# A transformer block's opening in another order, and its features dealt to partitions in fours

## The chip, the core and the metric

The kernel runs on one core of a Trainium2 chip. The metric is the time of one execution on the device, in microseconds, as the median of several runs. The engines are TensorE (PE, with its weight loads shown apart as PEld), VectorE (DVE), ScalarE (ACT), GpSimd (POOL) and SyncE (SP), which issues all transfers. Each engine executes its own list of instructions in order.

## The reference

A layer norm feeds attention with one shared key and value head, and an MLP with the mish activation; both are added to the input.

```
S, D, H, Dh, F = 2048, 512, 32, 16, 1792        # all float32
xn = (x - mean(x)) / sqrt(var(x) + 1e-5)
q, k, v = xn @ wq, xn @ wk, xn @ wv              # q: 32 heads of 16; k, v: one head
o = softmax(q @ k.T / 4) @ v                     # per head
h = xn @ w1 + b1
out = x + o @ wo + (h * tanh(softplus(h))) @ w2
```

## The kernel before

All engines' orders are written by hand; nothing is scheduled by a tool. The 2048 tokens form four chunks of 512 (c = 0 to 3), each of four tiles of 128 tokens by 512 features. Products of full precision are made of rounded parts: an operand is split in a high part (a copy that rounds) and a low part (the difference), and a product is three matmuls per 128 features, high by high, high by low and low by high.

The main part is run off a long table of letters (the loop over `word`): per step first scores whose maxima VectorE takes, second scores whose exponentials ScalarE takes, sums with the values, and halves of the MLP's products. The change does not touch the table. It touches the opening, the block under the pool `first`, up to `flush(*(("q", ...` near L876.

The opening loads tokens and weights, normalises the chunks, transposes them, makes keys and values, projects queries, and takes the 32 score maxima of the first unit of heads (u = 0).

- `load_tokens` (L311) loads a chunk's four tiles. `statistics` (L316) runs two instructions per tile on VectorE (L322, L323) and, after all four, `rooted` (L327): variance and mean in four columns (L329, L330) on VectorE, a logarithm and an exponential (L331, L332) on ScalarE. `root` (L335) refines the result with four small instructions, and `normalise` (L342) or `normalise_on_two` (L348) applies it, the latter with two tiles on VectorE and two on ScalarE (L354).
- `first_transposes` (L356) and `transposes` (L368) turn the normalised tiles on TensorE: the token tile is the weights, an identity the moving operand. There are 16 transposes for chunk 0 (L361) and 48 for the others (L375). ScalarE copies the high part out (L363, L377), and VectorE (chunks 0 and 1) or POOL (2 and 3) makes the low part (L387).
- `keys_values` (L408) multiplies with `wkv`; its rest, tagged `("v", c)`, transposes the values on VectorE (L427, four instructions, and a memset L428) when the tag is flushed.
- `queries` (L437) projects 128 of the 512 query columns. ScalarE evicts each (L448, L449), POOL makes the low part (L452), and SyncE stores it (L458, L459). There are four buffers `q`. The first one goes straight into `QS` with six transfers (L469). All weights of a query or MLP product come through three buffers `raw` (L254): a new load waits until the block that used the buffer before is split.
- `first_maxima` (L504) makes two score tiles (L490) and VectorE reduces them (L507). A loop over 32 of them (L832) puts transposes, keys, values and query products of later chunks between them. `fill_slot` makes so many matmuls of the next query or MLP product.
- After the 32, `place_maxima` (L516) writes the maxima through DRAM into two rows of `QS`: a store (L530) and two loads (L532), which wait for it on SyncE.

What sets the order around the change is the program text of the opening, since `later` and `flush` only move a step to the place where its tag is flushed.

Of the kernel before, what the change touches and what calls it, by code (L numbers as in the profile page):

```python
# [178 lines left out]
def attention_and_mlp(ctx: ExitStack, tc: tile.TileContext, x, wq, wk, wv, wo, w1, b1, w2, out):  # L179
# [73 lines left out]
    def raw_block(kind, i):  # L253
        raw = work.tile([P, D], F32, tag="raw", name=f"raw_{kind}{i}", bufs=RAWS)  # L254
        if kind in ("w1", "wq"):
            src = {"w1": w1, "wq": wq}[kind][:, i * P : (i + 1) * P].rearrange("(t p) f -> p t f", p=P)
            SP.dma_start(out=raw.rearrange("p (t f) -> p t f", t=DT), in_=src)
# [58 lines left out]
    def statistics(c, some=range(NT)):  # L316
        if some[0] == 0:
            ST[c] = first.tile([P, NT, 6], F32, tag="st", name=f"st{c}", bufs=2)
            MV[c] = first.tile([P, NT, 2], F32, tag="mv", name=f"mv{c}", bufs=2)
        st = ST[c]  # L320
        for t in some:
            DVE.bn_stats(out=st[:, t], in_=XS[c, t])  # L322
            DVE.bn_aggr(out=MV[c][:, t], in_=st[:, t])  # L323
        if len(some) == NT:
            rooted(c)
# [6 lines left out]
        ACT.activation(y, z, AF.Exp, scale=-0.5)  # L332
        ROOT[c] = v, y, z, m

    def root(c):  # L335
        v, y, z, m = ROOT[c]
        DVE.tensor_tensor(out=z, in0=y, in1=y, op=ALU.mult)
        DVE.tensor_tensor(out=z, in0=z, in1=v, op=ALU.mult)
        DVE.tensor_scalar(z, z, -0.5, 1.5, op0=ALU.mult, op1=ALU.add)
        DVE.tensor_tensor(out=y, in0=y, in1=z, op=ALU.mult)  # L340

    def normalise(c, engine, some=range(NT)):  # L342
        v, y, z, mean = ROOT[c]
        for t in some:
            x, m, r = XS[c, t], mean[:, t : t + 1], y[:, t : t + 1]
            engine.tensor_scalar(x, x, m, r, op0=ALU.add, op1=ALU.mult)

    def normalise_on_two(c):  # L348
        v, y, z, mean = ROOT[c]
        DVE.tensor_tensor(out=z, in0=y, in1=mean, op=ALU.mult)  # L350
        normalise(c, DVE, range(2))
        for t in range(2, NT):
            x, b, r = XS[c, t], z[:, t : t + 1], y[:, t : t + 1]
            ACT.activation(x, x, AF.Identity, bias=b, scale=r)  # L354

    def first_transposes():  # L356
        xt, FLAT[0] = x_tile(0, work)
        pts = [pair_bank(f"xt0_{k}") for k in range(2)]
        for t in (0, 2, 1, 3):
            for d in range(DT):  # L360
                PE.transpose(pts[d // 2][:, d % 2, t * P : (t + 1) * P], XS[0, t][:, d * P : (d + 1) * P], ident)  # L361
        for d in range(DT):
            ACT.activation(xt[:, 0, d], pts[d // 2][:, d % 2], AF.Copy)  # L363
            if d % 2:
                hi, lo = (xt[:, k, d - 1 : d + 1] for k in range(2))
                later(0, lambda hi=hi, lo=lo, pt=pts[d // 2]: below(DVE, lo, pt, hi), ("lo", 0))

    def transposes(c):  # L368
        xt, FLAT[c] = x_tile(c, first if c else work)
        n = 2 if c < 2 else 1  # L370
        for d in range(0, DT, n):
            pt = pair_bank(f"xt{c}_{d}")[:, :n]
            for a in range(n):
                for t in range(NT):
                    PE.transpose(pt[:, a, t * P : (t + 1) * P], XS[c, t][:, (d + a) * P : (d + a + 1) * P], ident)  # L375
            hi, lo = xt[:, 0, d : d + n], xt[:, 1, d : d + n]
            ACT.activation(hi, pt, AF.Copy)  # L377
            if c < 2:
                later(0, lambda hi=hi, lo=lo, pt=pt: below(DVE, lo, pt, hi), ("lo", c))
            else:  # L380
                x = slot_tile()
                ACT.activation(x, pt, AF.Copy)
                later(0, lambda hi=hi, lo=lo, x=x: below(POOL, lo, x, hi), ("lo", c))
            yield
# [131 lines left out]
    def place_maxima(u):  # L516
        m = work.tile([P, 2, 2, HG // 2 * NT], F32R, tag="mhl", name=f"mhl{u}", bufs=2)
        mt = work.tile([P, 32], F32, tag="mt", name=f"mt{u}", bufs=2)
        hi, lo = m[:, :, 0], m[:, :, 1]
        DVE.tensor_reduce(out=hi, in_=NMR[u][:, :, :, :1], axis=AX.X, op=ALU.max)  # L520
        DVE.tensor_reduce(
            out=NMR[u][:, :, :, 1], in_=hi.bitcast(F32).unsqueeze(3), axis=AX.X, op=ALU.max, negate=True
        )
        with nc.allow_low_precision(reason="one exact difference, rounded as it is written"):
            DVE.tensor_reduce(out=lo, in_=NMR[u], axis=AX.X, op=ALU.add)
        DVE.transpose(out=mt, in_=m.rearrange("p a k n -> p (a k n)").bitcast(F32))

        def send():
            d = scratch.tile([4, HG // 2 * NT, P], F32, tag="m", name=f"m{u}_dram", bufs=2)
            SP.dma_start(out=d.rearrange("r n (g k) -> g (r n) k", g=4), in_=mt)  # L530
            for a in range(2):
                SP.dma_start(  # L532
                    out=QS[u][a * 64 + 48 : a * 64 + 50].bitcast(F32),
                    in_=d[2 * a : 2 * a + 2].rearrange("r (pair t) k -> r pair (t k)", pair=2),
                )

        if u:
            return send
        send()

    PT = {}

# [188 lines left out]
    with tc.tile_pool(name="first", bufs=1) as first:  # L731
        load_tokens(0)
        wkv_raw = first.tile([P, DT, 2 * DH], F32, name="wkv_raw")
        for i, w in enumerate((wk, wv)):
            SP.dma_start(out=wkv_raw[:, :, i * DH : (i + 1) * DH], in_=w.rearrange("(t p) f -> p t f", p=P))
        first_queries = Piece(queries(0, 0))
        load_tokens(1)
        request("w1", 0, WB[0])
# [11 lines left out]
        def clear(*tiles):  # L750
            for t in tiles:
                t = t.rearrange("p a n -> p (a n)") if len(t.shape) == 3 else t
                ACT.activation(t, zero.to_broadcast(list(t.shape)), AF.Copy)
# [7 lines left out]
        def run(generator):  # L761
            for _ in generator:
                pass
# [334 lines left out]
```

## Time and profile before

| | us |
|---|---|
| median of three runs | 1558.04 (1556.52 to 1558.55) |
| the profiled execution | 1556.3 |
| its span, first to last instruction | 1554.5 |
| TensorE busy in the span | 1540.8 (99%) |
| VectorE, ScalarE, POOL busy | 1347.5, 1344.8, 861.0 |

A row of the timeline gives the start in us from the beginning of the span, the length, the engine, the line of the kernel, the operation, what it writes and reads, and how many instructions were merged. In brackets stands the idle time before it with what ended that. A row of the groups gives count, busy time, mean ns of one, and the idle time in front. The granted TensorE clock is 1.00 over the whole opening.

### The profile page before, as it was taken

To read this page: it belongs to the slowest core of one execution; us is meant where nothing else is said; L and a number is where in the kernel's file an instruction comes from. 1 tells how busy PE (TensorE), PEld (TensorE's weight loads), DVE (VectorE), ACT (ScalarE), POOL (GpSimd) and SP (SyncE) were. 2 spreads that over 40 slices of the span, in tenths; PEclk is the share of its full clock that TensorE was granted. 3 is DMA by queue.
4 is the path that set the end of the run, shared out by engine and by line. 5 is a ranking of instruction groups with operands and counts; after the bars stand their busy time and mean duration, and the time that the engine had idled before them with its cause. 6 is when DMAs were issued, how large, how long until landed. Compare 5 with 4: busy or idle time off the path is not lost.

```text
span 1554.5 us, 30222 instructions
## 1 busy us (share of the span) xinstructions
PE 1540.8 (99%) x11554; PEld 849.9 (55%) x11554; DVE 1347.5 (87%) x2291; ACT 1344.8 (87%) x2391; POOL 861.0 (55%) x749
## 2 busy tenths in 40 slices
PE   9899999999999999999999999999999999999998
PEld 7565554555555455545554555555555555555555
DVE  7759998899899898999988899999989999998841
ACT  6559999999899989897889989898889998888996
POOL 6657765677565455633556465734255663443652
PEclk9999999999999999999999999999999999999999
DMA  6773322332222222123333221213321221223120
GB/s 211 275 272 103 120 93 77 107 102 97 87 100 72 86 86 73 45 92 106 106 113 108 68 73 59 88 54 145 93 80 51 92 78 55 97 79 120 36 96 28
DMA packets 69399, 152.53 MB, mean 98 GB/s; under 512 B 12774, under 2 KB 22054, under 8 KB 68870
## 3 DMA queue, kind: packets, MB, share of 16 engines
q1 hardware_dynamic: 69254, 150.60, 29.3%
q8 instruction: 91, 1.49, 0.4%
q14 instruction: 54, 0.44, 0.1%
HBM read 98.51 MB, written 51.64 MB: 97 GB/s over the span
## 4 chain that ended last, share of the span: by engine, by line
PE 95%; POOL 1%; DVE 1%; ACT 1%; issue 1%; DMA 0%; SPq 0%; POOLq 0%; ACTq 0%; DVEq 0%
PE banks L556 32%; PE banks L926 23%; PE banks L552 19%; PE banks L490 18%; PE banks L699 1%; PE banks L412 1%; DVE nm L507 1%; PE banks L638 1%; PE banks L743 1%; DMA q_dram<-q 0%; POOL q L452 0%; PE banks L375 0%; ACT q L448 0%; DVE ysb L628 0%; POOL tn L679 0%
## 5 line engine op out<-in xcount | busy, mean ns | idle before, releaser
L502 DVE TENSOR_REDUCE nm<-banks 128x1 f32<-128x512 f32 x1984 | 1241.2, 683 | 131.2 <-PE banks L490 88.0
L991 ACT ACTIVATE pt<-banks 128x512 f32<-128x512 f32 x1594 | 858.3, 604 | 104.3 <-PE banks L552 49.8
L490 PE MATMUL banks<-KS,QS 48*128 48x512 f32 x2048 | 688.0, 423 | 2.5 <-DVE nm L507 2.2
L552 PE MATMUL banks<-QS,KS 64*128 64x512 f32 x2048 | 677.1, 417 | 0.2 <-ACT ty L936 0.2
L556 PE MATMUL banks<-pt,V 128*32 128x512 f32 x4096 | 536.0, 603 | 0.0
L552 PEld LDWEIGHTS banks<-QS,KS 64*128 64x128 f32 x2048 | 329.8, 185 | 224.5 <-DVE nm L502 110.4
L490 PEld LDWEIGHTS banks<-KS,QS 48*128 48x128 f32 x2048 | 329.2, 184 | 203.2 <-DVE nm L502 95.3
L926 PE MATMUL banks<-ring,act 64*128 64x512 f32 x1344 | 330.3, 397 | 0.1
L926 PE MATMUL banks<-X,wblk 64*128 64x512 f32 x1296 | 328.3, 396 | 0.3
L983 ACT ACTIVATE pt<-banks 128x1024 f32<-128x1024 f32 x227 | 230.7, 1027 | 37.1 <-PE banks L552 22.0
L926 PEld LDWEIGHTS banks<-X,wblk 64*128 64x128 f32 x1296 | 213.2, 185 | 28.8 <-issue 10.3
L926 PEld LDWEIGHTS banks<-ring,act 64*128 64x128 f32 x1344 | 211.5, 185 | 31.8 <-issue 11.4
L937 POOL TENSOR_TENSOR ysb<-ysb,ty 128x512 f32<-128x512 f32 x80 | 102.8, 1286 | 162.2 <-ACT ty L936 162.2
L556 PEld LDWEIGHTS banks<-pt,V 128*32 128x32 f32 x4096 | 85.9, 108 | 176.5 <-issue 167.5
L996 POOL TENSOR_SCALAR tu<-tu 128x512 f32<-128x512 f32 x54 | 80.3, 1487 | 125.5 <-ACT tu L995 125.4
L679 POOL TENSOR_TENSOR tn<-tn,tr 128x512 f32<-128x512 f32 x54 | 69.4, 1285 | 126.9 <-ACT tr L1001 126.9
L241 POOL TENSOR_TENSOR act<-th,act 128x512 fp32r<-128x512 f32 x56 | 72.1, 1287 | 99.8 <-ACT act L240 84.6
L682 POOL TENSOR_TENSOR th<-th,tn 128x512 f32<-128x512 f32 x56 | 72.2, 1290 | 0.0
L681 POOL TENSOR_TENSOR tz<-tz,tn 128x512 f32<-128x512 f32 x54 | 69.6, 1288 | 4.5
L998 POOL TENSOR_TENSOR tn<-tn,tu 128x512 f32<-128x512 f32 x54 | 69.5, 1287 | 4.5
L683 POOL TENSOR_TENSOR th<-th,tz 128x512 f32<-128x512 f32 x54 | 69.5, 1287 | 4.2
L926 PE MATMUL banks<-ring,ohl 64*128 64x512 f32 x288 | 64.3, 396 | 0.0
(112 smaller groups left out, 958.1 us busy)
## 6 DMA issues: line engine op xcount, KB each, us to landing
wblk<-w_dram SPq DMA_DIRECT2D x42, 512.0 KB
ring<-w_dram SPq DMA_DIRECT2D x42, 512.0 KB
QS<-q_dram SPq DMA_DIRECT2D x62, 192.0 KB
q_dram<-q SPq DMA_DIRECT2D x16, 512.0 KB
o_dram<-ov SPq DMA_DIRECT2D x31, 256.0 KB
raw_w<-in_B_w_dram SPq DMA_DIRECT2D x28, 256.0 KB
w_dram<-wblk SPq DMA_DIRECT2D x14, 512.0 KB
w_dram<-ring SPq DMA_DIRECT2D x14, 512.0 KB
```

The source lines that it names most:

```text
L241: POOL.tensor_tensor(out=lo, in0=src, in1=hi.bitcast(F32), op=ALU.subtract)
L490: PE.matmul(tile, QS[u][rows, pair, qt * P : (qt + 1) * P], KS[rows, kc * CT : (kc + 1) * CT], start=True, stop=True,)
L502: DVE.tensor_reduce(out=m[:, a : a + 1], in_=tile, axis=AX.X, op=ALU.max)
L552: PE.matmul(bank, KS[rows, kt * P : (kt + 1) * P], QS[u][rows, pair], start=True, stop=True)
L556: PE.matmul(BANK[7][h * 32 : (h + 1) * 32], V[:, kt], PT.pop((u * KT + kt) * HG + h), start=kt == 0, stop=kt == KT - 1,)
L681: POOL.tensor_tensor(out=z, in0=z, in1=n, op=ALU.subtract)
L682: POOL.tensor_tensor(out=h, in0=h, in1=n, op=ALU.mult)
L926: PE.matmul(self.p, w[rows], x[rows], start=self.first, stop=not any(self.todo))
L937: POOL.tensor_tensor(out=YS[t], in0=YS[t], in1=ty, op=ALU.add)
L983: ACT.activation(slots[slot // 2], banks[:, bank : bank + 2], AF.Exp, scale=SCALE)
L991: ACT.activation(PT[n], BANK[bank], AF.Exp, scale=SCALE)
L996: POOL.tensor_scalar_min(tu, tu, U_MAX)
```

## The change

*Features.* Tokens are loaded as before, a token to a partition. The weights with D rows (wk, wv, wq, w1) are loaded so that a partition holds four neighbouring rows instead of four rows 128 apart, and a transpose takes every fourth feature of the tile instead of 128 neighbours. So both operands agree as to which feature lies where.

*Order.* All three `QS` tiles are cleared at the start. Chunk 1's statistics are cut in two around chunk 0's low part; three of its tiles are normalised on VectorE, one on ScalarE. The second block of w1 is split behind that. Chunk 3's statistics move ahead of the maxima, two and two around chunk 1's low part, and its root follows the second maximum. The roots of chunks 2 and 3 run on POOL. The values are transposed behind maxima 7, 9 and 15 and behind all 32. The ones for `KS` are sent at maximum 22 instead of 26. The loads of the maxima follow their store after two fills of 12 matmuls.

```diff
-            src = {...}[kind][:, i * P : (i + 1) * P].rearrange("(t p) f -> p t f", p=P)
+            src = {...}[kind][:, i * P : (i + 1) * P].rearrange("(p t) f -> p t f", p=P)
...
-    def root(c):
+    def root(c, engine):
...
-    def normalise_on_two(c):
+    def normalise_on_two(c, n):
...
-                PE.transpose(pts[d // 2][...], XS[0, t][:, d * P : (d + 1) * P], ident)
+                PE.transpose(pts[d // 2][...], XS[0, t].rearrange("p (n d) -> p d n", d=DT)[:, d], ident)
...
-                    PE.transpose(pt[...], XS[c, t][:, (d + a) * P : (d + a + 1) * P], ident)
+                    PE.transpose(pt[...], XS[c, t].rearrange("p (n d) -> p d n", d=DT)[:, d + a], ident)
...
         if u:
-            return send
-        send()
+            return lambda: load(store())
+        d = store()
+        return lambda: load(d)
...
-            SP.dma_start(out=wkv_raw[...], in_=w.rearrange("(t p) f -> p t f", p=P))
+            SP.dma_start(out=wkv_raw[...], in_=w.rearrange("(p t) f -> p t f", p=P))
...
+        clear(*QT)
...
-        root(0)
-        normalise_on_two(0)
+        root(0, DVE)
+        normalise_on_two(0, 2)
...
-        statistics(1)
+        statistics(1, range(2))
         flush(("lo", 0))
-        split_block()
-        clear(*QT[:2])
+        statistics(1, range(2, NT))
+        rooted(1)
         run(first_keys)
...
-        root(1)
-        normalise_on_two(1)
+        root(1, DVE)
+        normalise_on_two(1, 3)
+        split_block()
...
-        clear(*QT[2:])
         statistics(2)
+        statistics(3, range(2))
         flush(("lo", 1))
         fill_slot(12)
-        root(2)
+        root(2, POOL)
         normalise(2, POOL)
+        statistics(3, range(2, NT))
...
-            if i < NT:
-                statistics(3, range(i, i + 1))
-            if i == NT + 1:
+            if i == 1:
                 rooted(3)
-            if i == NT + 3:
-                root(3)
+            if i == 7:
+                root(3, POOL)
                 normalise(3, POOL)
...
-            if i == 26:
+            if i == 22:
...
-            if i in (8, 12, 18, 22):
-                flush(("v", (8, 12, 18, 22).index(i)))
+            if i in (7, 9, 15):
+                flush(("v", (7, 9, 15).index(i)))
...
-        place_maxima(0)
-        for _ in range(NC * DT):
+        load_maxima = place_maxima(0)
+        flush(("v", 3))
+        for k in range(NC * DT):
             fill_slots(12)
+            if k == 1:
+                load_maxima()
```

Three places in the engines' lists follow. A row gives the line, the operation, what it writes and reads, its size, and how often it repeats. The numbers behind the names tell tiles apart.

VectorE around the start of the maxima, before (X_356 is chunk 1 transposed, z, v and y with 390 to 392 are chunk 2's root, pt_84 and pt_85 hold chunk 3's tokens):

```order
L387 TENSOR_TENSOR X_356<-banks,X_356 128x1024 x2
L337 TENSOR_TENSOR z_392<-y_391 128x4
L338 TENSOR_TENSOR z_392<-z_392,v_390 128x4
L339 TENSOR_SCALAR z_392<-z_392 128x4
L340 TENSOR_TENSOR y_391<-y_391,z_392 128x4
L507 TENSOR_REDUCE nm_441<-banks 128x2
L322 BN_STATS st_445<-pt_84 128x6
L323 BN_AGGR mv_446<-st_445 128x2
L507 TENSOR_REDUCE nm_441<-banks 128x2
```

VectorE at the same place in the change:

```order
L322 BN_STATS st_398<-pt_84 128x6
L323 BN_AGGR mv_399<-st_398 128x2
L387 TENSOR_TENSOR X_357<-banks,X_357 128x1024 x2
L322 BN_STATS st_398<-pt_85 128x6
L323 BN_AGGR mv_399<-st_398 128x2
L322 BN_STATS st_398<-pt_85 128x6
L323 BN_AGGR mv_399<-st_398 128x2
L507 TENSOR_REDUCE nm_451<-banks 128x2 x2
L329 TENSOR_SCALAR v_460<-mv_399 128x4
L330 TENSOR_SCALAR m_463<-mv_399 128x4
L507 TENSOR_REDUCE nm_451<-banks 128x2 x6
```

Chunk 2's root has gone to POOL, and chunk 3's statistics stand in front of the maxima instead of between them.

POOL behind the first split of w1, before (wblk_71 is the second block of w1, q_0 the first query product):

```order
L241 TENSOR_TENSOR wblk_70<-raw_w_110,wblk_70 128x512
L241 TENSOR_TENSOR wblk_71<-raw_w_202,wblk_71 128x512
L452 TENSOR_TENSOR q_0_308<-q_0_308 128x512
L387 TENSOR_TENSOR KS<-kvs_301,KS 16x512 x2
L241 TENSOR_TENSOR wq_213<-raw_wq_214,wq_213 128x256 x2
```

POOL at the same place in the change:

```order
L241 TENSOR_TENSOR wblk_70<-raw_w_110,wblk_70 128x512
L452 TENSOR_TENSOR q_0_307<-q_0_307 128x512
L241 TENSOR_TENSOR wblk_71<-raw_w_205,wblk_71 128x512
L387 TENSOR_TENSOR KS<-kvs_300,KS 16x512 x2
L241 TENSOR_TENSOR wq_216<-raw_wq_217,wq_216 128x256 x2
```

The second split of w1 has moved behind the first query's low part. The buffer that it frees is the one into which the last block of wq is loaded.

SyncE behind the last maxima, before:

```order
L458 DMA q_0_dram<-q_0_860 128x2x512
L459 DMA q_0_dram<-q_0_860 128x512
L530 DMA m_dram<-mt_902 4x32x32
L532 DMA QS_88<-m_dram 2x1024 x2
L458 DMA q_1_dram<-q_1_891 128x2x512
L459 DMA q_1_dram<-q_1_891 128x512
```

SyncE at the same place in the change:

```order
L530 DMA m_dram<-mt_897 4x32x32
L458 DMA q_1_dram<-q_1_886 128x2x512
L459 DMA q_1_dram<-q_1_886 128x512
L458 DMA q_2_dram<-q_2_916 128x2x512
L459 DMA q_2_dram<-q_2_916 128x512
L535 DMA QS_88<-m_dram 2x1024 x2
```

The two loads that wait for the maxima's store have moved behind the stores of two more query products.

More of the change, by code (lines that the diff above doesn't have):

```diff
@@ L255, in raw_block @@
         if kind in ("w1", "wq"):
-            src = {"w1": w1, "wq": wq}[kind][:, i * P : (i + 1) * P].rearrange("(t p) f -> p t f", p=P)
+            src = {"w1": w1, "wq": wq}[kind][:, i * P : (i + 1) * P].rearrange("(p t) f -> p t f", p=P)
             SP.dma_start(out=raw.rearrange("p (t f) -> p t f", t=DT), in_=src)
@@ L333, in rooted @@
         ROOT[c] = v, y, z, m
-    def root(c):
+    def root(c, engine):
         v, y, z, m = ROOT[c]
[L337 to L340, printed above, removed]
+        engine.tensor_tensor(out=z, in0=y, in1=y, op=ALU.mult)
+        engine.tensor_tensor(out=z, in0=z, in1=v, op=ALU.mult)
+        engine.tensor_scalar(z, z, -0.5, 1.5, op0=ALU.mult, op1=ALU.add)
+        engine.tensor_tensor(out=y, in0=y, in1=z, op=ALU.mult)
     def normalise(c, engine, some=range(NT)):
@@ L346, in normalise @@
             engine.tensor_scalar(x, x, m, r, op0=ALU.add, op1=ALU.mult)
-    def normalise_on_two(c):
+    def normalise_on_two(c, n):
         v, y, z, mean = ROOT[c]
         DVE.tensor_tensor(out=z, in0=y, in1=mean, op=ALU.mult)
-        normalise(c, DVE, range(2))
-        for t in range(2, NT):
+        normalise(c, DVE, range(n))
+        for t in range(n, NT):
             x, b, r = XS[c, t], z[:, t : t + 1], y[:, t : t + 1]
@@ L360, in first_transposes @@
             for d in range(DT):
-                PE.transpose(pts[d // 2][:, d % 2, t * P : (t + 1) * P], XS[0, t][:, d * P : (d + 1) * P], ident)
+                PE.transpose(pts[d // 2][:, d % 2, t * P : (t + 1) * P], XS[0, t].rearrange("p (n d) -> p d n", d=DT)[:, d], ident)
         for d in range(DT):
@@ L374, in transposes @@
                 for t in range(NT):
-                    PE.transpose(pt[:, a, t * P : (t + 1) * P], XS[c, t][:, (d + a) * P : (d + a + 1) * P], ident)
+                    PE.transpose(pt[:, a, t * P : (t + 1) * P], XS[c, t].rearrange("p (n d) -> p d n", d=DT)[:, d + a], ident)
             hi, lo = xt[:, 0, d : d + n], xt[:, 1, d : d + n]
@@ L526, in place_maxima, with store, load @@
         DVE.transpose(out=mt, in_=m.rearrange("p a k n -> p (a k n)").bitcast(F32))
-        def send():
+        def store():
             d = scratch.tile([4, HG // 2 * NT, P], F32, tag="m", name=f"m{u}_dram", bufs=2)
             SP.dma_start(out=d.rearrange("r n (g k) -> g (r n) k", g=4), in_=mt)
+            return d
+        def load(d):
             for a in range(2):
@@ L734, in attention_and_mlp @@
         for i, w in enumerate((wk, wv)):
-            SP.dma_start(out=wkv_raw[:, :, i * DH : (i + 1) * DH], in_=w.rearrange("(t p) f -> p t f", p=P))
+            SP.dma_start(out=wkv_raw[:, :, i * DH : (i + 1) * DH], in_=w.rearrange("(p t) f -> p t f", p=P))
         first_queries = Piece(queries(0, 0))
```

## The prediction

> **What bounds the kernel now.** I read the busy time by stretches first, then TensorE's timeline over the first 105 us, then the other engines' rows at each of its gaps.
>
> ```profile
> 200.00:1500.00 1300.00, 1299.74 (x10048) 701.58 (x10046) 1179.16 (x1993) 1160.04 (x2071) 711.33 (x611) 1.00 0.26 84
> ```
>
> The columns behind the length are PE, PEld, DVE, ACT, POOL, clock, DMA share and GB/s. The main part keeps TensorE busy 1299.74 of 1300 us and the change does not touch it. A microsecond won or lost in the opening therefore arrives at the end as one, and the opening alone has to be summed. TensorE executes the same matmuls in the same order before and after; only its waits, and the duration of its transposes, can differ. Its gaps:
>
> ```profile
> 19.32 3.02 PE L699 MATMUL banks<-X,wblk 128*128 128x512 f32 x12 [0.91 <-ACT q L448]
> 22.18 1.91 PE L375 MATMUL banks<-ident,pt 128*128 128x128 f32 x16
> 23.84 3.02 PE L699 MATMUL banks<-X,wblk 128*128 128x512 f32 x12
> ...
> 29.54 0.74 PE L490 MATMUL banks<-KS,QS 48*128 48x512 f32 x4
> ...
> 42.23 1.67 PE L699 MATMUL banks<-X,wq 128*128 128x512 f32 x6 [2.48 <-ACT q L448]
> ...
> 57.02 0.73 PE L699 MATMUL banks<-X,wq 128*128 128x512 f32 x2 [0.53 <-ACT q L448]
> 58.25 0.73 PE L490 MATMUL banks<-KS,QS 48*128 48x512 f32 x4 [0.49 <-DVE nm L507]
> ...
> 70.25 0.49 PE L490 MATMUL banks<-KS,QS 48*128 48x512 f32 x2 [0.44 <-DVE nm L507]
> 71.38 0.50 PE L490 MATMUL banks<-KS,QS 48*128 48x512 f32 x2 [0.63 <-DVE nm L507]
> ...
> 77.77 0.50 PE L490 MATMUL banks<-KS,QS 48*128 48x512 f32 x2 [0.62 <-DVE nm L507]
> ...
> 99.17 3.03 PE L699 MATMUL banks<-X,wq 128*128 128x512 f32 x12 [0.88 <-ACT q L448]
> ...
> 102.47 0.62 PE L552 MATMUL banks<-QS,KS 64*128 64x512 f32 x2
> ```
>
> After the first gap (0.91) these are 2.48, 1.02, 1.69 and 0.88 us, 6.07 together. That is the most the reordering can win.
>
> **The change, part by part.** *The 2.48 gap.* ScalarE sat in front of a root's logarithm whose variance VectorE had not finished:
>
> ```profile
> 24.31 2.36 DVE L387 TENSOR_TENSOR X<-banks,X 128x1024 fp32r<-128x1024 f32 x2 [1.54 <-ACT X L377]
> ...
> 31.25 0.68 DVE L322 BATCH_NORM_STATS2 st<-pt 128x6 f32<-128x512 f32 x1
> ...
> 40.08 0.16 DVE L329 TENSOR_SCALAR v<-mv 128x4 f32<-128x4 f32 x1
> ...
> 40.27 0.20 ACT L331 ACTIVATE z<-v 128x4 f32<-128x4 f32 x1 [3.04 <-DVE v L329]
> ...
> 41.58 0.60 ACT L448 ACTIVATE q<-banks 128x512 f32<-128x512 f32 x1
> ```
>
> The query eviction at 41.58 was queued behind it, and TensorE needed that bank. The change moves chunk 3's four statistics out from between the first maxima, two ahead of and two behind chunk 1's low part, and the variance to behind the second maximum. By the times worked out below, VectorE then has it at about 34.0; ScalarE evicts the first query behind the root, at 34.4 (0.3 us of wait for TensorE) and the second about when its product ends. I take 2.3 of the 2.48 as won.
>
> *What pays for it: a split is later, and a queue behind it.* The second block of w1 was split by POOL at once; now its split stands behind the first query's low part:
>
> ```profile
> 14.51 2.56 POOL L241 TENSOR_TENSOR wblk<-raw_w,wblk 128x512 fp32r<-128x512 f32 x2 [2.23 <-ACT wblk L240]
> 20.01 1.30 POOL L452 TENSOR_TENSOR q<-q 128x512 fp32r<-128x512 f32 x1 [2.94 <-ACT q L449]
> ...
> 28.93 3.03 POOL L346 TENSOR_SCALAR pt<-pt,m,y 128x512 f32<-128x512 f32 x4 [0.53 <-DVE y L340]
> ...
> 15.84 1.64 SPq L257 DMA_DIRECT2D raw_wq<-in_A_wq_dram  x2
> 17.52 2.65 SPq L314 DMA_DIRECT2D pt<-in_A_x_dram  x4
> 20.27 4.32 SPq L469 DMA_DIRECT2D QS<-q  x6
> ```
>
> There are three raw buffers, and the last wq block loads into the one this split frees. So SyncE waits until 21.4 + 1.28 = 22.7 rather than 17.1, and behind that wait stand chunk 3's four token loads and the six loads of QS that the first maxima need. With the issue times of these rows (about 0.45 each for wq and tokens, 0.6 for QS) the last QS load is issued at 28.4. I give it 2 us to land; the maxima's store, quoted further down, took at most 2.8 from the end of its issue (91.4) to the loads that wait for it (94.2), on a fuller queue. QS is then there at 30.5, against a first score at 29.54: **1.0 us lost**. VectorE is in the same place: tokens land at about 25.7 and 26.4, so two statistics (0.68 and some 0.1 of aggregate beyond it) end at 27.4, the low part (2.36) at 29.7, the other two at 31.4, two maxima at 33.7, the variance at 34.0. Low part and QS are late together, so the loss counts once. POOL is also 1.3 later and takes over the roots of chunks 2 and 3; chunk 2, normalised at 31.96 before, is ready at about 33.7 (four instructions of 4 columns, about 0.1 each) and wanted by the transposes at about 34.7. Net for the place: 2.3 - 0.3 - 1.0 = 1.0; since the earlier low part of chunk 0 and the lighter ScalarE queue work in its favour I take **1.2 won** (bounds -0.5 and 2.4).
>
> *The gaps from 57 to 78.* VectorE owes TensorE two maxima per step, and V transposes get between:
>
> ```profile
> L507 DVE TENSOR_REDUCE nm<-banks 128x2 f32<-128x1024 f32 x32 | 37.5, 1210 | 9.2 <-PE banks L490 9.1
> 67.70 2.11 PE L699 MATMUL banks<-X,wq 128*128 128x512 f32 x8
> ...
> 67.68 1.25 DVE L427 STREAM_TRANSPOSE V<-kvs 32x128 f32<-32x128 f32 x4
> ```
>
> One chunk costs 1.25 and a memset, 1.36 in all. Two maxima back to back take 2.3; a late step of TensorE takes 2.05 + 0.66 = 2.7. In the late steps nothing but the two clamps of fu is left, since V of chunk 2 moves to maximum 15 and V of chunk 3 behind all maxima: those 1.69 us go, I take 1.6. In the earlier steps TensorE takes 3.4 and VectorE with a V 3.66, so part of the 1.02 stays: 0.9 of it won, as chunk 3's root also leaves VectorE. **2.5 won** (bounds 1.0 and 2.7).
>
> *The maxima's loads.*
>
> ```profile
> 90.68 0.71 SPq L530 DMA_DIRECT2D m_dram<-mt  x1
> 94.23 0.57 SPq L532 DMA_DIRECT2D QS<-m_dram  x2
> ...
> 98.52 0.60 ACT L448 ACTIVATE q<-banks 128x512 f32<-128x512 f32 x1 [3.35 <-DMA q_dram<-q]
> ```
>
> SyncE stood 2.8 us (91.4 to 94.2) in front of the loads, with two query stores behind them, and ScalarE's eviction waited for such a store. The loads now follow two more stores, when the first has landed. The 0.88 gap goes: **0.9 won** (bounds 0 and 0.9). The loads still issue some 8 us before the first exponential's scores want these rows.
>
> *Nothing:* the three clears.
>
> ```profile
> 0.72 1.28 ACT L189 ACT_TABLE_LOAD   x1 [0.72 <-PEq L1084]
> 6.88 0.91 ACT L240 ACTIVATE wkv<-wkv_raw 128x192 fp32r<-128x192 f32 x4 [4.87 <-DMA wkv_raw<-in_A_wk_dram]
> L753 ACT ACTIVATE QS<-zero 128x1024 fp32r<-128x1024 f32 x3 | 3.1, 1051 | 0.0
> ```
>
> They run on ScalarE in the 4.87 us in which it waited for wkv; without that cover they would cost 3.1. The weights keep their bytes and their runs of 512 or 64 bytes.
>
> *The transposes* now read every fourth float of the token tile as weights, 64 times (16 + 48):
>
> ```profile
> L361 PE MATMUL banks<-ident,pt 128*128 128x128 f32 x16 | 1.9, 273 | 0.0
> L375 PE MATMUL banks<-ident,pt 128*128 128x128 f32 x48 | 7.0, 277 | 0.2
> L375 PEld LDWEIGHTS banks<-ident,pt 128*128 128x128 f32 x48 | 5.4, 140 | 2.6 <-issue 1.3 <-ACT pt L382 0.5 <-DVE nm L507 0.3
> L699 PE MATMUL banks<-X,wq 128*128 128x512 f32 x192 | 50.9, 402 | 3.9 <-ACT q L448 3.9
> L556 PE MATMUL banks<-pt,V 128*32 128x512 f32 x48 | 6.4, 605 | 0.0
> 83.62 14.66 PE L699 MATMUL banks<-X,wq 128*128 128x512 f32 x63
> L387 POOL TENSOR_TENSOR wq<-raw_wq,wq 128x256 fp32r<-128x256 f32 x2 | 1.4, 740 | 1.8 <-DVE wq L291 1.8
> ```
>
> This row is the change's unknown. Sixteen pairs of load and matmul took 22.18 to 23.84, 104 ns each. Either the matmul sets that pace and the load hides beside it, or the load does. For the matmul speaks that plain f32 streams slower than the rounded kind: 605 against 402 ns for 512 columns. No weight load of this trace has a step. Bounds: 0, where the load stays hidden; and a load at the pace of POOL's wq row, one of whose operands has a step of two floats, 740/256 = 2.9 ns an element: 128 x 2.9 = 0.37 us, 0.27 more than now, 64 x 0.27 = 17 us. I take 0, because the pair's own row is nearest.
>
> The Trainium skill speaks against the change here: "Advanced Engine Details and Errata", section SBUF Cachelines, has lines of 16 bytes, of which each needs two hits for full speed, and a step of four floats gives one. In "TensorE: Matmul & The Clock Gate", section LDWEIGHTS, 128 columns take an estimated 107 ns, close to the 104 here, so the load could be the pace; with both, the sum would be an estimated 2 us slower rather than 4.6 faster. No run here shows it yet.
>
> Sum: 1.2 + 2.5 + 0.9 = **4.6 us faster**. The profiled execution took 1556.3 (span 1554.5), so it becomes 1551.7; it lay 1.74 below the median of 1558.04, for which I say **1553.4**.
>
> **Rivals.** *The load's time doubles and sets the pace:* 208 ns a pair, 64 x 104 = 6.7 lost, net +2.1: 1560.1. For it: a load's 140 ns is longer than the pair's 104; against it the L556 row.
>
> *On the other side, slower:* the load falls to the 0.37 us above, 17 lost, net +12.4: 1570.4. It decides from 4.6/64 = 72 ns per transpose on, and beyond 120 ns the kernel is slower by over 0.2%. For it: no covering work, as the transposes stand in TensorE's own order; against it: the read would be far slower than the 0.42 ns a column of a 512-column moving read (14.66/63 = 0.23 us for 512).
>
> *The later split costs more:* loads of chunk 3 and QS share the DMA with the wq block, and QS lands at 33.5 instead of 30.5. Three of the 4.6 go: 1556.4. For it: the queue's order; against it: nothing else is issued in that time.
>
> *The gain is given back at the query stores,* whose four buffers also turn over through POOL's chain from 75 to 95: 2.5 won rather than 4.6 would leave 1555.5. Against it: two stores now leave 2.8 earlier.
>
> **The numbers.** Forecast 0.54 (its own range 1551.5 to 1555.2), load doubled or somewhat longer 0.19, split later 0.11, given back 0.06, far slower load 0.10. A difference counts as one from 0.2%, 3.1 us. Faster: most of the forecast and a little of the last two gains, 0.50. Slower: the far slower load and the worst of the doubled one, 0.15. Within: 0.35. The best sum of the bounds is 6.0 won, 1552.0; the lowest run before lay 1.5 under its median, so the range begins at 1550.6. It reaches 1561.2, past the doubled load, and leaves out the far slower one.
>
> **What would show it.** The pair of load and matmul in L375's run of 16: 104 ns if I am right, above 170 if not. The gap before the sixfold run of query products near 41 should be under 0.4, the first score near 30.5, no wait of SyncE between the maxima's store and the query stores, and TensorE's first exponential score at about 97.9 instead of 102.47. I am wrong if these hold and the time does not follow, or if the transposes are slower.

## The result and the profile after

The change takes 1553.79 us (median; 1552.17 to 1556.00) where the kernel before took 1557.26 (1555.61 to 1558.55) in the same comparison: ratio 0.998, 95% interval 0.9972 to 0.9987. That is 0.4 above the 1553.4 forecast, and 3.5 faster where the sum had said 4.6. The profiled execution took 1552.17 with a span of 1550.3, 4.2 below the span before. Executions of one kernel differ by up to 4 us, since in some of them the granted TensorE clock falls to 0.50 for a few microseconds of the opening, or tokens land later (both are shown below); in the profiled executions of before and of the change the clock is 1.00 throughout the opening, so the stages are compared in these.

The main part of the change, in the view of busy time by stretches (length, PE, PEld, DVE, ACT, POOL, clock, DMA share, GB/s), is what it was, so the opening alone decides:

```profile
200.00:1500.00 1300.00, 1299.76 (x10043) 700.95 (x10043) 1175.76 (x1987) 1159.62 (x2070) 710.07 (x610) 1.00 0.26 84
```

TensorE's timeline of the change, with the rows that answer to those shown of before (L699 has become L703, L552 has become L556):

```profile
22.12 2.08 PE L375 MATMUL banks<-ident,pt 128*128 128x128 f32 x16
23.96 3.01 PE L703 MATMUL banks<-X,wblk 128*128 128x512 f32 x12
...
29.89 0.73 PE L412 MATMUL banks<-X,wkv 128*128 128x512 f32 x2 [1.09 <-DVE X L387]
31.02 0.74 PE L412 MATMUL banks<-X,wkv 128*128 128x512 f32 x2 [0.40 <-DVE X L387]
31.69 0.73 PE L490 MATMUL banks<-KS,QS 48*128 48x512 f32 x4
...
42.33 1.65 PE L703 MATMUL banks<-X,wq 128*128 128x512 f32 x6 [0.49 <-ACT q L448]
...
57.39 0.73 PE L703 MATMUL banks<-X,wq 128*128 128x512 f32 x2 [0.49 <-ACT q L448]
...
81.14 17.38 PE L703 MATMUL banks<-X,wq 128*128 128x512 f32 x75
...
98.80 0.62 PE L556 MATMUL banks<-QS,KS 64*128 64x512 f32 x2
```

Both kernels run the same matmuls in the same order, so the distance between the same two instructions gives what a stage cost. The starts are those of these rows and of the rows in the prediction; "place 1" is the part that ends with the 2.48 gap:

| stage (us, starts before -> after) | before | after | difference | sum had said |
|---|---|---|---|---|
| to chunk 1's transposes (22.18 -> 22.12) | 22.18 | 22.12 | -0.06 | 0 |
| those transposes, to 23.84 -> 23.96 | 1.66 | 1.84 | +0.18 | 0 |
| place 1, to 42.23 -> 42.33 | 18.39 | 18.37 | -0.02 | -1.2 |
| to 57.02 -> 57.39 | 14.79 | 15.06 | +0.27 | 0 |
| late maxima, to 83.62 -> 81.14 | 26.60 | 23.75 | -2.85 | -2.5 |
| query stores and maxima's loads, to 102.47 -> 98.80 | 18.85 | 17.66 | -1.19 | -0.9 |

The differences add up to -3.67. The late stages brought what was forecast and a little more. Place 1 brought nothing in this execution: its gap of 2.48 has shrunk to 0.49, but two new waits of 1.09 and 0.40 stand before the first score, which starts at 31.69 instead of 29.54. They wait for chunk 1's low part, and VectorE's timeline of the change says why that is late:

```profile
26.30 0.69 DVE L322 BATCH_NORM_STATS2 st<-pt 128x6 f32<-128x512 f32 x1 [2.37 <-DMA pt<-in_A_x_dram]
...
27.82 0.70 DVE L322 BATCH_NORM_STATS2 st<-pt 128x6 f32<-128x512 f32 x1 [0.60 <-DMA pt<-in_A_x_dram]
...
28.65 2.32 DVE L387 TENSOR_TENSOR X<-banks,X 128x1024 fp32r<-128x1024 f32 x2
```

VectorE stood idle 2.37 + 0.60 us for chunk 3's tokens, with the low part queued behind their statistics. The tokens are late on SyncE's queue:

```profile
15.75 7.30 SPq L257 DMA_DIRECT2D raw_wq<-in_A_wq_dram  x2
23.10 2.04 SPq L314 DMA_DIRECT2D pt<-in_A_x_dram  x4
25.18 3.91 SPq L469 DMA_DIRECT2D QS<-q  x6
...
88.27 1.08 SPq L530 DMA_DIRECT2D m_dram<-mt  x1
...
92.57 1.89 SPq L535 DMA_DIRECT2D QS<-m_dram  x2
```

Two wq loads that took 1.64 us of SyncE before now take 7.30, because the second waits for the raw buffer that the late split of w1 frees. Chunk 3's tokens are issued from 23.10 instead of 17.52. The last two rows are the maxima's store and its loads, between which two query columns' stores now go out, where SyncE stood still before.

The transposes, in the view of groups, follow from the start to 125 us (count, busy us, mean ns, idle time):

```profile
L375 PEld LDWEIGHTS banks<-ident,pt 128*128 128x128 f32 x48 | 6.7, 208 | 2.3 <-ACT pt L382 0.8 <-issue 0.7 <-DVE nm L507 0.4
```

The strided weight load takes 208 ns instead of 140, and a run of 16 takes 115 ns each (22.12 to 23.96) instead of 104.

### The profile page after: what moved, and what is told of

Same layout as the page of the kernel before. It is cut to its first block, busy times and chain, and to the rows that moved or that the text cites. A ratio compares the mean times of both kernels' runs of the same rounds, so it can differ in the third digit from the quotient of the medians.

```text
span 1550.3 us, 30223 instructions
## 1 busy us (share of the span) xinstructions
PE 1540.4 (99%) x11554; PEld 850.3 (55%) x11554; DVE 1346.3 (87%) x2284; ACT 1343.6 (87%) x2390; POOL 862.3 (56%) x757
## 4 chain that ended last, share of the span: by engine, by line
PE 97%; DVE 1%; DMA 1%; ACT 0%; issue 0%; POOL 0%; SPq 0%; ACTq 0%; POOLq 0%; DVEq 0%
PE banks L560 32%; PE banks L934 23%; PE banks L556 19%; PE banks L490 18%; PE banks L703 3%; PE banks L642 1%; DMA pt<-in_A_x_dram 1%; PE banks L412 0%; PE banks L375 0%; DVE ysb L632 0%; POOL wblk L241 0%; DVE X L387 0%; ACT X L363 0%; DVE st L322 0%; PE banks L361 0%
## 5 line engine op out<-in xcount | busy, mean ns | idle before, releaser
L556 PE MATMUL banks<-QS,KS 64*128 64x512 f32 x2048 | 677.6, 418 | 0.2 <-ACT ty L944 0.2
L556 PEld LDWEIGHTS banks<-QS,KS 64*128 64x128 f32 x2048 | 330.0, 184 | 224.8 <-DVE nm L502 110.4
```

The lines of the kernel that those rows point to most:

```text
L556: PE.matmul(bank, KS[rows, kt * P : (kt + 1) * P], QS[u][rows, pair], start=True, stop=True)
```

## The experiments

Theory after the result: the order wins its 2.5 in the late maxima and 1.2 at the stores as forecast; at place 1 the reordering is good for about 2, and the late split gives it back through SyncE's queue; the transposes cost 0.7 in all. The rivals are that the transposes ate place 1's gain, that the split's new place on POOL and ScalarE did, or that the loads and values were hidden anyway. All ratios are against the kernel before.

### Four kernels: order and features apart, with and without the early split

*The order alone* has the weights and transposes as before:

```diff
-            src = {...}[:, i * P : (i + 1) * P].rearrange("(p t) f -> p t f", p=P)
+            src = {...}[:, i * P : (i + 1) * P].rearrange("(t p) f -> p t f", p=P)
...
-                PE.transpose(pts[...], XS[0, t].rearrange("p (n d) -> p d n", d=DT)[:, d], ident)
+                PE.transpose(pts[...], XS[0, t][:, d * P : (d + 1) * P], ident)
```

The edit is the same in L375 and for wk and wv.

> The changed kernel with the features laid out as before, so only the order is new. Theory (a load with a step of four floats takes 209 instead of 140 ns, of which 11 ns a pair reach TensorE, and the first of a burst some 90): L375's pairs return to 109 ns, the main part starts 0.8 to 1.3 us earlier than 98.80, at 97.5 to 98.0. Rival (the features' layout pays for itself by faster loads of wk and wv): wkv's split begins later, at 6.9 instead of 6.63, and the main part starts at 98.8 or later.

Measured: 1552.56, ratio 0.9977 (0.9967 to 0.9987), span 1550.2. TensorE's timeline of it:

```profile
24.12 3.02 PE L703 MATMUL banks<-X,wblk 128*128 128x512 f32 x12
...
42.13 1.66 PE L703 MATMUL banks<-X,wq 128*128 128x512 f32 x6 [0.50 <-ACT q L448]
```

Place 1 takes 42.13 - 24.12 = 18.01, against 18.37 with the features and 18.39 before. So the transposes did not eat the gain there: without them all but 0.4 is still missing. The first exponential score came at 98.42, 0.4 earlier than in the change and not at the 97.5 to 98.0 expected, and the span is only 0.1 shorter, so little of the layout's cost shows in the whole.

*The features alone* are the same edit the other way on the kernel before.

> The kernel before with the features dealt out in fours and nothing else. Theory: 0.7 to 1.3 us slower than before in the profile (64 pairs at 120 instead of 109 ns, and some 90 ns at each burst's head), of which the waits that stood in the opening may hide a part; no change of the first maxima or of the loads. Rival (the layout brings something): not slower, or faster.

Measured: 1557.46, ratio 0.9998 (0.9989 to 1.0007), span 1554.2. TensorE's timeline of it:

```profile
21.74 2.08 PE L375 MATMUL banks<-ident,pt 128*128 128x128 f32 x16
23.58 3.01 PE L699 MATMUL banks<-X,wblk 128*128 128x512 f32 x12
...
41.96 1.67 PE L699 MATMUL banks<-X,wq 128*128 128x512 f32 x6 [2.39 <-ACT q L448]
```

The run of 16 costs 1.84 here too, yet the loss of 0.7 to 1.3 that was expected did not come; the rival, "not slower", did. Place 1, with 16 transposes in it, takes 18.38 against 18.39, since the large wait at its end (2.39 instead of 2.48) takes up part of what they cost. Also, the first transposes start at 9.72 instead of 10.23; that is not put down to the features, as two executions of the change itself have 9.91 and 10.23. In the stages the transposes' cost shows where no wait stands behind it: of the two kernels below without that wait, the one with the new features needs 0.24 more for place 1.

*The early split* keeps the change and puts the one line back to where the buffer comes free early:

```diff
         flush(("lo", 0))
+        split_block()
         statistics(1, range(2, NT))
...
         normalise_on_two(1, 3)
-        split_block()
```

> The second block of w1 is split right behind chunk 0's low part again, the rest is the changed kernel. Theory (the late split holds back chunk 3's tokens and QS on SyncE, and with them chunk 1's low part): SyncE issues the last wq block at about 17 instead of 22.5, the two waits of the keys' products for chunk 1's low part (1.09 and 0.40 us) go, and the first score starts at 29.6 to 30.0 instead of 31.69. The exponentials of the main part then start 1.5 to 2.0 us earlier than 98.80, and the time is 1.5 to 2.0 us under the changed kernel's. Rival (what is won at 30 us is lost again where TensorE waited before, at the second query product near 42 us or at the query stores behind 85 us): first score at 30, but the main part still starts at 98.3 to 98.8.

Measured: 1550.78, ratio 0.9961 (0.9949 to 0.9974). In the profiled execution the clock was 0.50 from about 12 to 15 us, so only what lies behind that can be compared:

```profile
26.43 3.01 PE L703 MATMUL banks<-X,wblk 128*128 128x512 f32 x12
...
42.80 1.65 PE L703 MATMUL banks<-X,wq 128*128 128x512 f32 x6 [0.49 <-ACT q L448]
```

Place 1 takes 42.80 - 26.43 = 16.37, 2.00 less than in the change. The two waits for the low part are gone. The first exponential score, at 99.26, follows the start of place 1 by 72.83, where it was 74.84 in the change: the 2.0 at the upper end of what was expected.

*Early split and features as before together:*

> Both of the former: early split and features as before, the new order otherwise. If the two costs are apart in time they add: main part at 95.8 to 96.5, 2.3 to 3.0 us under the changed kernel and 6.3 to 7.0 under the one before. Rival (the query stores behind 85 us have become the bound): the start is not below 97.3 and TensorE shows a wait for the query eviction behind 85 us.

Measured: 1549.65 (1549.61 to 1549.88), ratio 0.9952 (0.994 to 0.9965), span 1548.0: the lowest median of these kernels, below both the change and the kernel before. TensorE's timeline of it:

```profile
23.75 3.02 PE L703 MATMUL banks<-X,wblk 128*128 128x512 f32 x12
...
39.88 1.66 PE L703 MATMUL banks<-X,wq 128*128 128x512 f32 x6 [0.50 <-ACT q L448]
```

Place 1 takes 39.88 - 23.75 = 16.13, 2.26 less than before: the 2.3 of the prediction, with nothing to pay for it. The wait of 5.7 us on SyncE is gone: its two wq loads take 1.63 us. The first exponential score comes at 96.18, within the 95.8 to 96.5 expected.

### The late split with a buffer of its own for the last wq block

An early split changes two things, SyncE's wait and the order on POOL and ScalarE. Here the order of all engines is that of the change, and the last wq block alone gets a landing buffer in the opening's pool, so that its load waits for nobody:

```diff
-        raw = work.tile([P, D], F32, tag="raw", name=f"raw_{kind}{i}", bufs=RAWS)
+        pool_, n, tag = (first, 1, "raw3") if (kind, i) == ("wq", 3) else (work, RAWS, "raw")
+        raw = pool_.tile([P, D], F32, tag=tag, name=f"raw_{kind}{i}", bufs=n)
```

> The changed kernel with one buffer more: the last query weight block (wq, block 3) loads into a landing buffer of its own, so its load no longer waits on SyncE until POOL has split the second block of w1. The split itself stays as late as in the change, and every engine's order stays the same. Theory (the late split costs time only because SyncE's queue, with chunk 3's tokens and QS's stores, stands behind that wait of 5.7 us): the wq loads take about 1.6 us on SyncE instead of 7.3, the token loads are issued at about 17.5 instead of 23.1, VectorE does not wait for tokens, the first score starts at 29.3 to 29.8 instead of 31.69, the sixfold run of query products near 42.3 starts at about 40, and the whole is 2.0 to 2.5 us faster than the change (span near 1548). Rival (the split's place on POOL and ScalarE costs, by pushing the rest of their queues 1.3 us back): SyncE's wait goes, but the start at 42.3 moves by under 0.5 and the span stays at 1550.

Measured: 1550.21, ratio 0.9954 (0.9939 to 0.9969), span 1548.5. SyncE and TensorE of it (lines one further down):

```profile
16.03 1.23 SPq L258 DMA_DIRECT2D raw_wq<-in_A_wq_dram  x2
17.30 2.93 SPq L315 DMA_DIRECT2D pt<-in_A_x_dram  x4
```

```profile
24.21 3.01 PE L704 MATMUL banks<-X,wblk 128*128 128x512 f32 x12
...
29.89 0.74 PE L491 MATMUL banks<-KS,QS 48*128 48x512 f32 x4
...
40.58 1.66 PE L704 MATMUL banks<-X,wq 128*128 128x512 f32 x6 [0.49 <-ACT q L449]
```

The first score starts at 29.89, before it no wait is left, and place 1 takes 16.37, just as with the early split. So between these executions the wait on SyncE is the whole cost of the late split, 18.37 - 16.37 = 2.0 us; its place on POOL and ScalarE costs nothing that shows. The two starts missed what was expected by a little (29.8 at the latest, and about 40).

*The change as it is,* on the same chip:

> The changed kernel as it is, beside the others of this job on the same chip: 1552.2 in an execution whose TensorE clock is 1.00 throughout (span 1550.3), and 1.4 to 4 us more in those in which the clock is halved for 3.4 us in the opening.

Measured: 1553.94, ratio 0.9981 (0.9972 to 0.999), span 1550.7. It repeats the result: place 1 takes 18.19 in its profile. Its median lies 3.7 above that of the kernel with the own buffer, though, and not 2.0. The profiled execution of another kernel, the one with the old values below, shows a part of the rest. Up to this row it has the order of the change, and its clock is still 1.00:

```profile
31.20 0.73 PE L412 MATMUL banks<-X,wkv 128*128 128x512 f32 x2 [2.26 <-DVE X L387]
```

TensorE waits 2.26 here and not 1.09, and the first score starts at 32.99, although SyncE issued chunk 3's tokens only 0.16 later: the second one was there at 29.13 rather than 27.82. In the six profiled executions that have the change's place for the statistics and the late split, that token was there by 27.1 at the earliest and at 29.1 at the latest. So 2.0 is the late split's cost in one execution; in others the tokens land over 1 us later. Why they do is open.

### One part of the order taken back at a time

These three take one part out of the change. The clock fell in the opening of all of their profiled executions, so their totals say little; what is compared lies where the clock was 1.00.

*Chunk 3's statistics* go back between the maxima:

```diff
-        statistics(3, range(2))
...
-        statistics(3, range(2, NT))
...
-            if i == 1:
-                rooted(3)
+            if i < NT:
+                statistics(3, range(i, i + 1))
+            if i == NT + 1:
+                rooted(3)
```

> The changed kernel with chunk 3's statistics between the first maxima again and the variance behind the sixth, late split kept. Theory: chunk 1's low part no longer waits for tokens, so the first score comes at 30.0 to 30.8 instead of 31.69; but ScalarE waits for the variance again and the query product at 42.33 starts at 42.5 to 43.5 with a wait of 1.5 to 2.5 us. So the place as a whole is worth 0.3 to 1.2 us. Rival (the statistics in front cost what they bring): start of the query product at 42.0 to 42.4.

Measured: 1557.12, ratio 0.9998 (0.9989 to 1.0008), span 1554.9. VectorE and TensorE of it:

```profile
24.24 2.36 DVE L387 TENSOR_TENSOR X<-banks,X 128x1024 fp32r<-128x1024 f32 x2 [0.52 <-ACT X L377]
```

```profile
31.09 1.20 PE L490 MATMUL banks<-KS,QS 48*128 48x512 f32 x4 [1.60 <-DMA QS<-q]
...
45.66 2.08 PE L703 MATMUL banks<-X,wq 128*128 128x512 f32 x6 [2.38 <-ACT q L448]
```

The gap is back, 2.38 against 0.49, so moving the statistics takes 1.9 out of it. The low part runs at 24.24, since no token has to be there first, and still the first score starts at 31.09, now waiting for `QS`. Both things that the late split holds up were late by nearly the same amount, as the prediction had it; bringing the low part forward alone wins 0.6, so that the move nets about 1.3 while the split is late. The starts themselves missed what was expected (30.0 to 30.8 for the first score, 42.5 to 43.5 for the query product): `QS` came later, and the clock was 0.50 from 33.0 to 36.5, between the two rows, so the length of the place is not compared.

*The values* go back to maxima 8, 12, 18 and 22:

```diff
-            if i in (7, 9, 15):
-                flush(("v", (7, 9, 15).index(i)))
+            if i in (8, 12, 18, 22):
+                flush(("v", (8, 12, 18, 22).index(i)))
...
-        flush(("v", 3))
```

> The changed kernel with the values transposed behind maxima 8, 12, 18 and 22 as before. Theory (the waits of 0.44, 0.63 and 0.62 us at 70 to 78 came from the transposes between late maxima): two or three such waits return, the main part starts 1.5 to 2.3 us later, at 100.3 to 101.1. Rival (they went because the roots and statistics left VectorE): under 0.5 us later.

Measured: 1558.39, ratio 1.0005 (0.9995 to 1.0014), span 1556.0. TensorE of it:

```profile
60.21 0.73 PE L703 MATMUL banks<-X,wq 128*128 128x512 f32 x2 [0.50 <-ACT q L448]
61.33 0.73 PE L490 MATMUL banks<-KS,QS 48*128 48x512 f32 x4 [0.39 <-DVE nm L507]
...
73.36 0.50 PE L490 MATMUL banks<-KS,QS 48*128 48x512 f32 x2 [0.44 <-DVE nm L507]
74.49 0.50 PE L490 MATMUL banks<-KS,QS 48*128 48x512 f32 x2 [0.62 <-DVE nm L507]
...
80.89 0.50 PE L490 MATMUL banks<-KS,QS 48*128 48x512 f32 x2 [0.62 <-DVE nm L507]
...
86.75 13.53 PE L703 MATMUL banks<-X,wq 128*128 128x512 f32 x58
```

Four waits for the maxima return, where two or three were expected, and the stage takes 86.75 - 60.21 = 26.54, against 23.75 in the change and 26.60 before. The values' places are worth 2.8, the whole of that stage.

*The maxima's loads* go back behind their store, in two runs:

```diff
-        load_maxima = place_maxima(0)
+        place_maxima(0)()
...
-            if k == 1:
-                load_maxima()
```

> The changed kernel with the maxima's loads right behind their store. Theory (SyncE's wait held back the query stores and these the query buffers): SyncE stands 2.5 to 3 us in front of the loads, and TensorE waits 0.7 to 1.2 us for a query eviction near 95 us; the main part starts at 99.6 to 100.0 instead of 98.80. Rival (the other gains had freed enough slack): no such wait, start at 98.8.

> The changed kernel with the maxima's two loads issued by SyncE directly behind their store again, as before the change, run a second time because the clock was halved for 6.8 us in the first profile. Theory (SyncE stands in front of these loads until the store has landed, and two query stores and ScalarE's eviction wait behind it): a gap of about 1 us on TensorE near 96 and one of some 0.4 near 101 come back, 1.2 to 1.5 us slower than the change (span near 1551.7 with the clock at 1.00). Rival (these loads were hidden anyway): the gaps do not come back and the span stays at 1550.3.

Measured: 1556.55, ratio 0.9998 (0.9988 to 1.0007), and 1555.94, ratio 0.9991 (0.9982 to 1.0001); spans 1555.8 and 1555.0. SyncE and TensorE of the second:

```profile
91.73 1.07 SPq L530 DMA_DIRECT2D m_dram<-mt  x1
95.13 0.57 SPq L535 DMA_DIRECT2D QS<-m_dram  x2
```

```profile
84.60 14.66 PE L703 MATMUL banks<-X,wq 128*128 128x512 f32 x63
...
100.05 3.02 PE L703 MATMUL banks<-X,wq 128*128 128x512 f32 x12 [0.78 <-ACT q L448]
...
103.33 0.62 PE L556 MATMUL banks<-QS,KS 64*128 64x512 f32 x2
```

SyncE stands still from 92.80 to 95.13 again, ScalarE's eviction waits, and the stage takes 103.33 - 84.60 = 18.73 instead of 17.66: 1.1 us. The first of the two runs has 18.73 as well. So the loads were not hidden before; the second gap that was expected near 101 did not come.

### Weight loads with a step, measured by themselves

In the warm-up the transposes read a cleared `QS` tile as weights, nine each with a step of 2, 3, 4, 6 and 8 floats (the start of the opening therefore waits longer for the clear):

```diff
-            PE.transpose(idle[...], ident, ident)
+            step = (1, 1, 1, 2, 3, 4, 6, 8)[i // 9]
+            PE.transpose(idle[...], wide[:, : step * P].rearrange("p (n s) -> p s n", s=step)[:, 0], ident)
```

> The changed kernel, whose warm-up transposes take a cleared tile as weights with steps of 1 (27 times), 2, 3, 4, 6 and 8 floats (9 times each), so that the load is measured by itself. Theory (two elements per 16-byte line are enough): loads of step 1 and 2 take 140 ns, pairs 109; from step 4 on 209 and 120, no more at 6 and 8; step 3 between. Rival (the cost grows with the step): 2 dearer than 1, 8 dearer than 4, pairs of step 8 above 150 ns. The time of the whole is not of interest: the warm-up starts later and is 18 longer.

Measured: one execution, 1556.53, span 1554.6. Busy time by stretches for this line alone, one stretch for each step from 2 to 8 (length, PE, PEld, clock, DMA share, GB/s):

```profile
8.82:9.89 1.07, 1.07 (x11) 1.07 (x10) 1.00 0.91 329
9.89:10.92 1.03, 1.03 (x11) 1.03 (x10) 1.00 1.15 304
10.92:12.00 1.08, 1.08 (x11) 1.08 (x10) 1.00 0.83 89
12.00:13.23 1.23, 1.23 (x11) 1.23 (x10) 1.00 0.20 19
13.23:14.13 0.90, 0.90 (x11) 0.90 (x9) 1.00 0.68 200
```

Nine starts fall in each of the first four stretches: 119, 114, 120 and 137 ns a transpose at steps 2, 3, 4 and 6. The last stretch goes from the first to the ninth start, 0.90/8 = 112 ns at step 8. The 27 at step 1 are no base for these: they took 207 ns each, from 3.22 to 8.82, and the warm-up of the kernel before is as slow until about 7 us (6 or 7 of them in a microsecond, 11 behind 8 us), without any difference in the clock column. The last 22 of that warm-up, from 7.83 to 10.23, took 109 each. So step 4 costs 11 ns here, as it does in the run of 16 (115 against 104). The cost does not grow with the step: 6 is the worst and 8 the cheapest. Nor does it go with the transfers running beside it, whose share was lowest at step 6. So neither the theory (no cost at 2, the same from 4 on) nor its rival came true. It is one execution with the steps always in this order, so differences of a few nanoseconds between steps are not shown.

## Why the prediction came out as it did

*The bound and the late stages* were right. The main part kept its pace, and 3.67 of the 4.2 us in the span lie in TensorE's waits and transposes of the opening. The late maxima won 2.85 where 2.5 stood, 2.8 of it from the values' places. The maxima's loads won 1.19 where 0.9 stood, and SyncE's queue shows no pause between the store and the query stores behind it, as foretold. The first exponential's scores came at 98.80 rather than 97.9.

*The step that failed is the price of the late split,* "1.0 us lost" in a place said to win 1.2. Its mechanism was right to the queue and the buffer: SyncE waits, chunk 3's tokens and `QS` come late, and low part and `QS` are late together. The size was off: the own buffer shows 2.0, and executions in which the tokens land later lose more. Both landings were put too early. The tokens were issued from 23.10 rather than 22.7 and the two that VectorE waited for were there at 26.30 and 27.82 rather than 25.7 and 26.4; so the low part ended at 30.97 rather than 29.7, and the first score started at 31.69 rather than 30.5. `QS`, seen alone in the kernel with the old statistics, was there at 31.09 rather than 30.5. That leaves the gap: 2.3 of it was to be won, 1.99 was (2.48 to 0.49). The remaining 0.49 is an eviction that ScalarE does behind the transposes' copies, which the prediction had put under 0.4. The 0.3 that the net sum took off, a wait of TensorE behind ScalarE's first query eviction, did not show: that eviction ran at 35.45, later than the 34.4 foretold, and no wait stands in TensorE's rows from the first score to the 0.49. POOL's later queue cost nothing either.

*The transposes* were the other term with a wrong size: 0 was taken, 0.7 is what 64 of them cost at 11 ns. The sentence "104 ns if I am right, above 170 if not" left out what happened. The load grew by half, from 140 to 208 ns, but most of it lies beside the matmul. The prediction's argument, that the matmul's own pace covers the load, holds for all but 11 ns of the 68. By the Trainium skill ("Advanced Engine Details and Errata", SBUF Cachelines) a read that meets each 16-byte line once is slowed; the load's 208 ns at a step of 16 bytes agrees, but 119 ns a transpose at a step of 8 bytes and 112 at one of 32, against 109 without a step, do not follow from it. The forecast's estimated loss by that rule, a sum 2 us slower rather than 4.6 faster, did not come. (The 0.42 ns a column that the prediction sets against the far slower load is 0.45 by its own row, 14.66/63/512; no term rests on it.)

*What met in the total.* Place 1 fell short by 1.2 and the transposes of chunk 1 and the stage to 57.39 by 0.45; the late stages gave 0.6 more, and the rest of the span over 0.5 (4.2 in the span against the 3.67 of the table). Of that, 0.3 lies between the first exponential score and the first product with the values, which took 6.70 us before and 6.38 after; the rest is open. So misses of 1.6 and gains of 1.2 beyond the sum met, and 4.2 came in the profiled executions where 4.6 was foretold; in the medians 3.5 came. That the time still came within 0.4 of the forecast is in part luck: the kernel before had a median of 1557.26 beside the change, 0.8 less than the 1558.04 from which the forecast was counted, and that took back most of the 1.1 by which the gain fell short.

*The rivals.* The doubled and the far slower load fell by the 115 ns. "Given back at the query stores" fell by the stage's 17.66. "The later split costs more" was the right direction; `QS` was not as late as its 33.5.

## What to carry to other kernels

Moving a step that frees a buffer moves every transfer that stands behind the load into that buffer on the same queue, also those that have nothing to do with it; count the landing of the last of them, not the issue of the first, and allow for landings that differ by over 1 us from one execution to the next. When a stage gains nothing although its gap is closed, look for the new wait a little ahead of it. A cost that vanishes in a test by itself may only have been taken up by a wait, and comes back once that wait is gone.

## What was not expected of the hardware

The granted clock can fall to half behind a short wait. Busy time by stretches of the kernel with the loads taken back, second run, cut in steps of 3.41 us that meet the moments at which its clock changed:

```profile
27.47:30.88 3.41, 1.37 (x7) 0.80 (x5) 2.09 (x4) 0.21 (x1) 3.05 (x8) 1.00 0.71 204
30.88:34.30 3.42, 3.42 (x9) 1.47 (x9) 2.89 (x6) 1.05 (x2) 2.83 (x4) 0.50 0.65 241
```

The clock holds for stretches of 3.41 us. In the profiled openings there are six falls, for one or two stretches each; in the stretch in front of them TensorE was busy for 1.03 and 1.93 us (old statistics), 1.36 (early split), 1.37 and 1.38 (loads taken back) and 2.07 (old values). The Trainium skill ("TensorE: Matmul & The Clock Gate", What's actually happening) has free-running windows of 3413 ns and a fall to half after an idle one; the length agrees, but here no window was idle, and a wait of 1.6 to 2.4 us was enough. It is not certain to: in the profiled execution of before, the stretch with the 2.48 gap had 1.64 of 3.42 busy and the next one kept 1.00:

```profile
38.10:41.52 3.42, 1.64 (x11) 1.02 (x9) 2.21 (x4) 1.22 (x4) 0.50 (x1) 1.00 0.31 106
41.52:44.93 3.41, 2.70 (x12) 1.75 (x13) 0.56 (x1) 2.26 (x5) 2.32 (x2) 1.00 0.21 66
```

So a wait in the opening can cost more than itself, if the windows happen to fall that way. The kernels with the early split or the own buffer have no wait of over 1 us behind their first transposes, and none of their profiled executions has a fall there. That their waits are too short to lower the clock fits, but was not tried by itself. Where the limit lies stays open: two stretches with 1.93 and 1.94 us busy (order alone, features alone) were not followed by a fall either, and none with more than 2.07 was.
